# Folding the gate and noise columns of an MLP into its second weight matrix, over two steps per weight tile

## The chip, the cores and the metric

The kernel runs on one core of a Trainium2 chip, in one launch. The metric is device time in microseconds (us). The kernel before takes 1118.16 us, the median of three runs (1114.34 to 1119.37).

Five engines run their own instruction lists in order and meet only at semaphores: PE (TensorE, matmuls and transposes, which write PSUM), ACT (ScalarE, activations and copies), DVE (VectorE, elementwise work), POOL (GpSimd, here elementwise subtractions and products) and SP, which issues most DMA transfers.

## The reference, cut to what matters

Three layers follow one another on 3072 tokens (4 batches of 768) with 384 channels:

```python
state = alpha[t] * state + outer(k[t], v[t]);  y[t] = q[t] @ state   # 8 heads of 48
h = x @ w_in;  g = h * sigmoid(h);  x2 = g @ w_out                    # 384 -> 2048 -> 384
logits = x2 @ w_gate;  noise_scale = log1p(exp(x2 @ w_noise))         # 384 -> 8 experts
noisy = logits + noise_scale * noise                                  # top 2, softmax weights
out[t] = sum over its two experts of weight * relu(x2 @ w1[e]) @ w2[e]
```

The product `x2 @ w_gate` is `g @ (w_out @ w_gate)`. The kernel therefore folds the gate and noise matrices (16 columns together, called `wgn`) into `w_out` once, and the second matmul of the MLP gives 384 output columns and 16 gate and noise columns at a time.

## The kernel before

Attention works on chunks of 128 tokens, 24 of them; the MLP works on blocks of 384 tokens (three chunks), eight of them, each in 16 steps, one for each 128 rows of the hidden layer. The order of every engine's work is the order in which the program is written (`manual_schedule`): nothing is reordered.

**Attention in units.** `stage1_units` is a generator that gives a chunk in five units: unit 0 (transposed keys `kts`, score matmuls, masked scores `am`), unit 1 (`unit_kv`: new state `S`), unit 2 (first half of `y`), unit 3 (second half of `y`, copied to `xr` by ACT), unit 4 (`xr` transposed, split into `xh` and `xl`). Before the loop over MLP steps, 15 units (three chunks) run: the prelude. After that each step of the MLP runs one unit.

**Steps of the MLP.** Step m of block j runs `l1(j, m)` (nine matmuls of 384 columns), then the pointwise part `act1` (ACT `th`, DVE `gf`, ACT `gh`, POOL `gl`), then a unit of attention, then `l2(j, m-2)` (nine matmuls of 400 columns).

**Weights.** `w_in` and `w_out` come as raw 64 bit words, 64 tiles of loading in all, of which 32 are prepared: 9 in the prelude, then two in each step of block 0 (steps 0 to 10, and one in step 11). `narrow` turns a raw tile (`wraw`) into float (`wf`) by three DVE instructions (L142 to L144); `split` gives a high part by ACT and the low part by a subtraction on POOL (both L137 and L138). After each `narrow` the next raw load is issued on SP; with n buffers of `wraw` it waits for the n-th narrow before its own use.

**The fold.** A `w_out` tile that was narrowed waits in the list `folds`. `fold()` takes it: three transposes on PE (L96), a copy to `St` on ACT (L371), a product with `wgn` on PE (L374), a copy of the 16 columns to `wo_h` on ACT (L375), and the remainder to `wo_l` on DVE (L376). Then come the `th` of this step and the narrows. Folds stand at the end of each prelude chunk and right behind `l1` in each step of block 0. `St` has one buffer, which `unit_kv` also uses for its sum (L263, L264).

Of the kernel before, what the change touches and what calls it, by code (L numbers as in the profile page):

```python
# [8 lines left out]
F32 = mybir.dt.float32  # L9
F32R = mybir.dt.float32r  # L10
BF = mybir.dt.bfloat16
I32 = mybir.dt.int32
U32 = mybir.dt.uint32
AF = mybir.ActivationFunctionType
# [7 lines left out]
DM = H * D  # L22
# [10 lines left out]
KD = DM // 128  # L33
# [21 lines left out]
def attention_mlp_moe(ctx: ExitStack, tc: tile.TileContext, aqk, vt, win, wout, wgn, noise, w12,  # L55
# [3 lines left out]
    PE, DVE, ACT, POOL = nc.tensor, nc.vector, nc.scalar, nc.gpsimd  # L59
# [10 lines left out]
    s1 = s1c.enter_context(tc.tile_pool(name="s1", bufs=2, side="right"))  # L70
    stg = s1c.enter_context(tc.tile_pool(name="stg", bufs=1, side="right"))
# [3 lines left out]
    p1 = p1c.enter_context(tc.tile_pool(name="p1", bufs=3, space=PSUM))  # L75
# [3 lines left out]
    def load_chunk(c):  # L79
        t = s1.tile([PR, AL + 2 * NP * C], F32, name="aqk", bufs=3)  # L80
        if c:
            nc.sync.dma_start(t, aqk[c])
        else:
            nc.sync.dma_start(t[:, :AL], aqk[c, :, :AL])
            nc.scalar.dma_start(t[:, AL:], aqk[c, :, AL:])
        aqk_t[c] = (t[:, :AL], *[t[:, AL + i * NP * C:AL + (i + 1) * NP * C].rearrange("p (a b) -> p a b", a=NP)
                                 for i in range(2)])
        x = s1.tile([C, H, D], F32, name="v", bufs=3)
        nc.sync.dma_start(x, vt[c])
        v_t[c] = x  # L90
# [3 lines left out]
    def flip(o, x):  # L94
        n = x.shape[0]
        PE.transpose(o, x, ident[:n, :n])  # L96

    jp = stg.tile([128, DM], I32, name="wf", bufs=3)[:, :128]
    POOL.iota(jp, pattern=[[1, 128]], base=0, channel_multiplier=-1)
    ident = const.tile([128, 128], F32)  # L100
    DVE.tensor_scalar(ident, jp, 0.0, None, op0=OP.is_equal)
# [21 lines left out]
    raw = {}  # L123

    def load_w(src, m):
        t = stg.tile([128, DM, 2], I32, name="wraw", bufs=4)
        nc.sync.dma_start(t.rearrange("p n w -> p (n w)"), src[m])
        return t

    def load_win(m):  # L130
        raw["i", m] = load_w(win, m)

    def load_wout(m):
        raw["o", m] = load_w(wout, m)
# [3 lines left out]
        (eng or DVE).tensor_tensor(l, r, h.bitcast(F32), OP.subtract)  # L138

    def narrow(t, pool=None):  # L140
        f = (pool or stg).tile([128, DM], I32, name="wf", bufs=3)
        DVE.tensor_scalar(f, t[:, :, 1], 3, 0x3fffffff, op0=OP.logical_shift_left, op1=OP.bitwise_and)  # L142
        DVE.scalar_tensor_tensor(f, t[:, :, 1], -0x40000000, f, op0=OP.bitwise_and, op1=OP.bitwise_or)
        DVE.scalar_tensor_tensor(f, t[:, :, 0], 29, f, op0=OP.logical_shift_right, op1=OP.bitwise_or)  # L144
        return f.bitcast(F32)
# [54 lines left out]
    def prep_a(c):  # L200
        al = aqk_t[c][0]
        P = s1.tile([PR, NP, CP], F32, name="P", bufs=1)
        R = s1.tile([PR, NP, CP], F32, name="R", bufs=1)
        P_t[c] = (P, R)
        DVE.tensor_tensor_scan(P.rearrange("p a b -> p (a b)"), al[:, :AL - 1], past[:, :AL - 1], 1.0, OP.mult, OP.add)
        DVE.tensor_scalar(rc, P[:, :, C], 1e-30, None, op0=OP.max)
        DVE.reciprocal(rc, rc)
        for k in range(2):
            ACT.activation(junk, al, AF.Relu, bias=neg[:PR], scale=1.0 - 2.0 * k, accum_out=amx[:PR, k, c:c + 1])
        POOL.tensor_copy(rcs[:PR, c], rc)  # L210
# [122 lines left out]
    def unit():  # L333
        next(gen, None)
# [6 lines left out]
    def wl(n=1):  # L341
        for _ in range(n):
            if wloads:
                kind, m = wloads.pop(0)
                (load_win if kind == "i" else load_wout)(m)

    def wn():
        if wpreps:
            k = wpreps.pop(0)
            f = narrow(raw.pop(k))  # L350
            wl()
            return k, f
# [6 lines left out]
            if kind == "o":  # L359
                folds.append((m, f))  # L360

    folds = []

    def fold():
        while folds:
            m, f = folds.pop(0)
            p = p1.tile([128, KD, 128], F32, name="ps1")
            for k in range(KD):
                flip(p[:, k], f[:, k * 128:(k + 1) * 128])
            t = s1.tile([128, KD, 128], F32, name="St", bufs=1)  # L370
            ACT.activation(t, p, AF.Copy)  # L371
            p = p1.tile([128, 2 * E], F32, name="ps1")
            for k in range(KD):
                PE.matmul(p, t[:, k], wgn_t[:, k], start=(k == 0), stop=(k == KD - 1))  # L374
            ACT.activation(wo_h[:, m, DM:], p, AF.Copy)  # L375
            DVE.tensor_sub(wo_l[:, m, DM:], p, wo_h[:, m, DM:].bitcast(F32))  # L376

    wl(2)
    load_chunk(2)
    wl(2)  # L380
    prep_a(0)
    prep_b(0)
    prep_c(0)
# [1 line left out]
    nc.scalar.dma_start(nz, noise)  # L385
    for i in range(15):
        unit()
        if i % 5 == 4:
            fold()

    def range_load(i):
        raw["r", i] = load_w(win if i < MF else wout, i % MF)
# [245 lines left out]
    for i in range(NS + LAG):  # L638
        if i < NS:
            j, m = divmod(i, MF)  # L640
# [34 lines left out]
            if j == 0:  # L675
                fold()
                for _ in range(2):
                    w = wn()
                    step(ac)
                    wh(w)  # L680
                    step(ac)
            else:
                run(ac)
            if m < MF - 1 and j < NB - 1:
                unit()
        if i >= LAG:
            j, m = divmod(i - LAG, MF)
# [18 lines left out]
    p1 = w3c.enter_context(tc.tile_pool(name="p3", bufs=2, space=PSUM))  # L706
# [65 lines left out]
    for i in range(NS + LAG):  # L772
        if i < NS:
            q, f = divmod(i, FF)
# [5 lines left out]
            if q + 1 < len(groups):  # L780
                ne, ng = groups[q + 1]
                nt = len(GR[ng][1])
                t = f - (FF - 1 - nt)
# [16 lines left out]
        if i >= LAG:  # L800
            q, f = divmod(i - LAG, FF)
# [16 lines left out]
    with tc.If(bad != 0), ExitStack() as fc:  # L818
# [8 lines left out]
        with tc.For_i(0, B, 1) as b, tc.For_i(0, NP, 1) as pr:  # L827
            for s in range(2):
# [11 lines left out]
                for x in range(2):  # L840
                    p = pl.tile([128, 512], F32, name="ph")
# [3 lines left out]
                for e in range(D):  # L845
                    u = fw.tile([D, S], F32, name="fu")
                    w = fw.tile([D, S], F32, name="fs")
                    for x in range(2):
                        h = slice(x * HS, (x + 1) * HS)
                        p = pl.tile([128, 512], F32, name="ph")  # L850
# [14 lines left out]
        for src, dst in ((win, wt[0]), (wout, wt[1])):  # L865
            for m in range(MF):
                t = fw.tile([128, DM, 2], I32, name="fraw")
                nc.sync.dma_start(t.rearrange("p n w -> p (n w)"), src[m])
                f = narrow(t, fw)
                x = fw.tile([128, DM], F32, name="fx")  # L870
                DVE.tensor_scalar(x, t[:, :, 1].bitcast(F32), 1e4, None, op0=OP.mult)
                sq = fw.tile([128, DM], F32, name="fsq")
                DVE.tensor_tensor(sq, x, x, OP.mult)
                DVE.scalar_tensor_tensor(dst[:, m], sq, (2.0 ** -15 * 1.125 * 1e4) ** 2, f,
                                         op0=OP.is_ge, op1=OP.mult)
        with tc.For_i(0, B, 1) as b, tc.For_i(0, NCB, 1) as c:
# [5 lines left out]
            for m in range(MF):  # L882
                p = pl.tile([128, 512], F32, name="ph")
# [9 lines left out]
            p = fps.tile([128, KD, C], F32, name="ft")  # L893
# [3 lines left out]
            p = fps.tile([128, 2 * E], F32, name="fl")  # L897
# [9 lines left out]
            for e in range(E):  # L907
# [3 lines left out]
                for f in range(FF):  # L911
                    p = pl.tile([128, 512], F32, name="ph")
# [79 lines left out]
```

## Time and profile before

| what | value |
|---|---|
| median of three runs | 1118.16 us |
| profiled execution | 1118.28 us |
| its span, first to last instruction | 1116.5 us |
| PE busy over the span | 1055.8 us, 95% |
| DVE busy | 586.5 us, 53% |
| ACT busy | 395.1 us, 35% |
| POOL busy | 260.0 us, 23% |
| mean granted clock of PE | 0.979 of full speed |

The shares are means over the whole span. The stretch that the change touches is the first 165 us: the prelude up to about 64 us, and block 0 up to about 165 us. In what follows the stretch is read by itself: busy time in windows, who waited for whom in it, and the single instructions in order of time. A row of the timeline gives start, length, engine, line, operation, output and inputs, and in brackets the idle time of the engine before it and who ended that.

### The profile page before, as it was taken

To read this page: it belongs to the slowest core of one execution; us is meant where nothing else is said; L and a number is where in the kernel's file an instruction comes from. 1 tells how busy PE (TensorE), PEld (TensorE's weight loads), DVE (VectorE), ACT (ScalarE), POOL (GpSimd) and SP (SyncE) were. 2 spreads that over 40 slices of the span, in tenths; PEclk is the share of its full clock that TensorE was granted. 3 is DMA by queue.
4 is the path that set the end of the run, shared out by engine and by line. 5 is a ranking of instruction groups with operands and counts; after the bars stand their busy time and mean duration, and the time that the engine had idled before them with its cause. 6 is when DMAs were issued, how large, how long until landed. Compare 5 with 4: busy or idle time off the path is not lost. (4 is left out here: it accounts for less than half of the span.)

```text
span 1116.5 us, 16697 instructions
## 1 busy us (share of the span) xinstructions
PE 1055.8 (95%) x6323; PEld 1020.6 (91%) x6323; DVE 586.5 (53%) x1335; ACT 395.1 (35%) x837; POOL 260.0 (23%) x252
## 2 busy tenths in 40 slices
PE   4768889999999999999999998999999999999995
PEld 3668889999999999999999988999999999999995
DVE  6766664666768777686647452244333243324220
ACT  2233344333343333434335423244333333323221
POOL 4334441031301303122020222211222222221212
PEclk9998889999999999999999998999999999999998
DMA  7333387243532325222023243445444435353313
GB/s 224 95 117 91 121 276 229 88 154 117 185 104 75 118 85 167 77 85 66 1 85 111 85 135 66 103 93 151 120 86 103 101 74 129 69 123 77 42 16 38
DMA packets 55225, 119.64 MB, mean 107 GB/s; under 512 B 6640, under 2 KB 33648, under 8 KB 55136
## 3 DMA queue, kind: packets, MB, share of 16 engines
q1 hardware_dynamic: 43456, 97.23, 28.9%
q0 software_dynamic: 11264, 20.68, 10.2%
q8 instruction: 52, 0.85, 0.3%
q10 hardware_dynamic: 416, 0.58, 0.2%
q14 instruction: 37, 0.30, 0.1%
HBM read 82.22 MB, written 36.24 MB: 106 GB/s over the span
## 5 line engine op out<-in xcount | busy, mean ns | idle before, releaser
L744 PE MATMUL acc<-w3h,hx 128*128 128x384 f32 x832 | 241.9, 342 | 0.7 <-ACT y L754 0.7
L725 DVE SCALAR_TENSOR_TENSOR hx<-ph,hx 128x64 fp32r<-128x64 f32 (+1 forms) x192 | 79.2, 443 | 289.1 <-ACT hx L721 280.5
L756 POOL DMA_INDIRECT out_dram<-y,xrow x64 | 98.5, 1538 | 348.5 <-ACT y L754 284.7
L721 ACT ACTIVATE hx<-ph 128x448 fp32r<-128x448 f32 (+1 forms) x128 | 65.4, 517 | 262.8 <-PE ph L718 179.8
L744 PEld LDWEIGHTS acc<-w3h,hx 128*128 128x128 f32 x832 | 153.4, 189 | 4.3 <-ACT y L754 1.0
L744 PE MATMUL acc<-w3l,hx 128*128 128x384 f32 x448 | 150.2, 335 | 0.0
L471 PE MATMUL acc<-wo_h,gh 128*128 128x400 f32 x384 | 143.7, 374 | 0.0
L718 PE MATMUL ph<-xh,w3h 128*128 128x384 f32 (+1 forms) x384 | 136.0, 354 | 3.6 <-DVE hx L725 3.5
L718 PE MATMUL ph<-xh,w3l 128*128 128x384 f32 (+1 forms) x384 | 135.3, 352 | 0.0
L718 PE MATMUL ph<-xl,w3h 128*128 128x384 f32 (+1 forms) x384 | 135.0, 352 | 0.0
L471 PE MATMUL acc<-wo_l,gh 128*128 128x400 f32 x384 | 134.3, 350 | 0.0
L471 PE MATMUL acc<-wo_h,gl 128*128 128x400 f32 x384 | 134.1, 349 | 0.0
L444 PE MATMUL ph<-xh,win_h 128*128 128x384 f32 x384 | 131.7, 343 | 0.0
L444 PE MATMUL ph<-xl,win_h 128*128 128x384 f32 x384 | 130.5, 340 | 0.0
L444 PE MATMUL ph<-xh,win_l 128*128 128x384 f32 x384 | 130.5, 340 | 0.0
L451 ACT ACTIVATE th<-ph 128x384 f32<-128x384 f32 x128 | 62.6, 489 | 162.9 <-PE ph L444 155.1
L454 DVE SCALAR_TENSOR_TENSOR gf<-th,ph 128x384 f32<-128x384 f32 x128 | 70.5, 551 | 76.9 <-ACT th L451 75.3
L461 DVE TENSOR_TENSOR gl<-gf,gh 128x384 fp32r<-128x384 f32 x112 | 72.3, 646 | 66.3 <-ACT gh L459 61.6
L459 ACT ACTIVATE gh<-gf 128x384 fp32r<-128x384 f32 x128 | 67.2, 525 | 110.1 <-DVE gf L454 102.5
L744 PEld LDWEIGHTS acc<-w3l,hx 128*128 128x128 f32 x448 | 81.2, 181 | 0.7
L718 PEld LDWEIGHTS ph<-xh,w3h 128*128 128x128 f32 x384 | 72.5, 189 | 6.9 <-issue 4.2
L471 PEld LDWEIGHTS acc<-wo_h,gh 128*128 128x128 f32 x384 | 74.0, 193 | 2.7 <-issue 0.4
(141 smaller groups left out, 1747.0 us busy)
## 6 DMA issues: line engine op xcount, KB each, us to landing
wraw<-in_w_dram SPq DMA_DIRECT2D x64, 384.0 KB, 4.6
aqk<-in_aqk_dram SPq DMA_DIRECT2D x23, 674.2 KB, 5.4
wraw<-in_win_dram SPq DMA_DIRECT2D x32, 384.0 KB, 3.9
wraw<-in_wout_dram SPq DMA_DIRECT2D x32, 384.0 KB, 3.4
xrow<-xd SPq DMA_DIRECT2D x48, 196.5 KB, 3.4
xd<-pad SPq DMA_DIRECT2D x12, 589.5 KB, 11.4
v<-in_v_dram SPq DMA_DIRECT2D x24, 192.0 KB, 5.8
xd<-pad SPq DMA_DIRECT2D x4, 786.0 KB, 15.1
```

The lines of the kernel that those rows point to most:

```text
L444: PE.matmul(p, w[:, m, k], x[:, k], start=(n == 0), stop=(n == 3 * KD - 1))
L451: ACT.activation(th, p, AF.Tanh, scale=0.5)
L454: DVE.scalar_tensor_tensor(g, th, 1.0, p, op0=OP.add, op1=OP.mult)
L459: ACT.activation(gh, g, AF.Copy)
L461: (POOL if j == 0 else DVE).tensor_tensor(gl, g, gh.bitcast(F32), OP.subtract)
L471: PE.matmul(ACC[j][i], g[:, sl], w[:, m], start=(m == 0 and n == 0), stop=(m == MF - 1 and n == 2))
L718: PE.matmul(p[:, :N], w[:, k, fs], x[:, k], start=(n == 0), stop=(n == 3 * KD - 1))
L721: ACT.activation(hx[:, :N], p[:, :N], AF.Relu)
L725: DVE.scalar_tensor_tensor(hx[:, o:o + b - a], p[:, a:b], 0.0, hx[:, a:b].bitcast(F32), op0=OP.max, op1=OP.subtract)
L744: PE.matmul(AC3[e, g][t][:m], hx[:, o:o + m], w[:, f], start=(f == 0 and q == 0), stop=(f == FF - 1 and q == len(prods) - 1))
L756: st = POOL.indirect_dma_start(out=out, out_offset=bass.IndirectOffsetOnAxis(ap=x[:n, RW - 1:].bitcast(I32), axis=0), in_=y[a:a + n], in_o ...
```

## The change

`fold()` is cut in two. A call first finishes the tile that the call before had begun (product with `wgn`, copy to `wo_h`, remainder to `wo_l`), and then begins the next one (transposes and copy). The copy goes to a buffer of its own, `ft`, and not to `St`. The list `mids` holds the tile in between. A call takes one tile, where it took all that were in the list. In the prelude the calls move from the end of each chunk to units 0 and 2 of chunks 1 and 2. `wf` gets a fourth buffer and `wraw` gives one up, so that three raw loads are outstanding instead of four.

```diff
-    jp = stg.tile([128, DM], I32, name="wf", bufs=3)[:, :128]
+    jp = stg.tile([128, DM], I32, name="wf", bufs=4)[:, :128]
...
-        t = stg.tile([128, DM, 2], I32, name="wraw", bufs=4)
+        t = stg.tile([128, DM, 2], I32, name="wraw", bufs=3)
...
-        f = (pool or stg).tile([128, DM], I32, name="wf", bufs=3)
+        f = (pool or stg).tile([128, DM], I32, name="wf", bufs=4)
...
-    folds = []
+    folds, mids = [], []
 
     def fold():
-        while folds:
-            m, f = folds.pop(0)
-            p = p1.tile([128, KD, 128], F32, name="ps1")
-            for k in range(KD):
-                flip(p[:, k], f[:, k * 128:(k + 1) * 128])
-            t = s1.tile([128, KD, 128], F32, name="St", bufs=1)
-            ACT.activation(t, p, AF.Copy)
+        if mids:
+            m, t = mids.pop(0)
             p = p1.tile([128, 2 * E], F32, name="ps1")
             for k in range(KD):
                 PE.matmul(p, t[:, k], wgn_t[:, k], start=(k == 0), stop=(k == KD - 1))
             ACT.activation(wo_h[:, m, DM:], p, AF.Copy)
             DVE.tensor_sub(wo_l[:, m, DM:], p, wo_h[:, m, DM:].bitcast(F32))
+        if folds:
+            m, f = folds.pop(0)
+            p = p1.tile([128, KD, 128], F32, name="ps1")
+            for k in range(KD):
+                flip(p[:, k], f[:, k * 128:(k + 1) * 128])
+            t = stg.tile([128, KD, 128], F32, name="ft")
+            ACT.activation(t, p, AF.Copy)
+            mids.append((m, t))
 
     wl(2)
     load_chunk(2)
-    wl(2)
+    wl(1)
...
-        if i % 5 == 4:
+        if i % 5 in (0, 2) and i > 4:
             fold()
```

On PE, in step 3 of block 0, between the last matmul of `l1` and the second half of `y`, the order before is: transposes of the `w_out` tile (from `wf`), product with `wgn` (from `St`), `y`.

```order
 L444 MATMUL ph<-xh,win_l 128x384
 L96 MATMUL ps_694<-ident,wf 128x128 x3
 L374 MATMUL ps_700<-wgn_t,St 128x16 x3
 L275 MATMUL ps_665<-S,aqk 128x96
 L279 MATMUL ps_665<-v,am 128x48 x2
```

At the same place of the changed kernel the product comes first, and its input is `ft`.

```order
 L447 MATMUL ph<-xh,win_l 128x384
 L369 MATMUL ps_686<-wgn_t,ft 128x16 x3
 L96 MATMUL ps_692<-ident,wf 128x128 x3
 L275 MATMUL ps_657<-S,aqk 128x96
 L279 MATMUL ps_657<-v,am 128x48 x2
```

The product now belongs to the tile whose transposes stood in the step before; the transposes belong to the next one.

On ACT, from the end of step 8 to step 9 (unit 3 in between, as after step 3), before: the split of the second weight (`win_h`), the copy `xr` of unit 3, the fold's copy `St` and its `wo_h`, then step 9's `th` and first split.

```order
 L137 ACTIVATE win_h<-wf 128x384
 L282 ACTIVATE xr<-ps_1012 128x384
 L371 ACTIVATE St<-ps_1102 128x384
 L375 ACTIVATE wo_h<-ps_1108 128x16
 L451 ACTIVATE th<-ph 128x384
 L137 ACTIVATE wo_h<-wf 128x384
```

The same engine at the same place in the changed kernel:

```order
 L137 ACTIVATE win_h<-wf 128x384
 L282 ACTIVATE xr<-ps_1004 128x384
 L370 ACTIVATE wo_h<-ps_1094 128x16
 L378 ACTIVATE ft<-ps_1100 128x384
 L454 ACTIVATE th<-ph 128x384
 L137 ACTIVATE wo_h<-wf 128x384
```

`wo_h` moved ahead of the copy, so nothing of this fold stands between `xr` and it on ACT.

On PE, where the prelude ends, before: last matmul of `y`, transposes of `xr`, the whole fold of the last tile of the prelude, then the first `l1`.

```order
 L279 MATMUL ps_458<-v,am 128x48 x2
 L96 MATMUL ps_474<-ident,xr 128x128 x3
 L96 MATMUL ps_480<-ident,wf 128x128 x3
 L374 MATMUL ps_486<-wgn_t,St 128x16 x3
 L444 MATMUL ph<-xh,win_h 128x384
```

The changed kernel at the same place, up to the keys of the next chunk:

```order
 L96 MATMUL ps_478<-ident,xr 128x128 x3
 L447 MATMUL ph<-xh,win_h 128x384
 L447 MATMUL ph<-xl,win_h 128x384
 L447 MATMUL ph<-xh,win_l 128x384
 L447 MATMUL ph<-xh,win_h 128x384
 L447 MATMUL ph<-xl,win_h 128x384
 L447 MATMUL ph<-xh,win_l 128x384
 L447 MATMUL ph<-xh,win_h 128x384
 L447 MATMUL ph<-xl,win_h 128x384
 L447 MATMUL ph<-xh,win_l 128x384
 L369 MATMUL ps_494<-wgn_t,ft 128x16 x3
 L96 MATMUL ps_536<-ident,aqk 128x112 x4
```

The second half of that fold moved behind the nine matmuls of the first `l1`.

## Rows read from the trace of the kernel before

**Rows 1.** Windows: start:end, length, busy PE, PEld, DVE, ACT, POOL, clock, DMA.

```profile
60.00:165.00 105.00, 85.33 (x466) 79.77 (x467) 68.03 (x127) 39.46 (x96) 43.44 (x44) 0.85 0.49 149
165.00:200.00 35.00, 35.00 (x225) 34.60 (x225) 14.45 (x29) 13.50 (x30) 7.08 (x9) 1.00 0.71 207
```

**Rows 2.** Waits of DVE, 60 to 165 us: total, times, longest.

```profile
DVE wo_l L376 <- ACT wo_h L375: 28.7, 13, 4.8
...
DVE gf L454 <- ACT th L451: 2.0, 2, 1.7
```

**Rows 3.** Timeline of DVE: last instruction of each narrow, steps 0 to 5.

```profile
70.67 0.56 DVE L144 SCALAR_TENSOR_TENSOR wf<-wraw,wf 128x384 int32<-128x384 int32 x1
...
77.35 0.56 DVE L144 SCALAR_TENSOR_TENSOR wf<-wraw,wf 128x384 int32<-128x384 int32 x1
...
79.99 0.56 DVE L144 SCALAR_TENSOR_TENSOR wf<-wraw,wf 128x384 int32<-128x384 int32 x1
...
86.60 0.56 DVE L144 SCALAR_TENSOR_TENSOR wf<-wraw,wf 128x384 int32<-128x384 int32 x1
...
89.25 0.56 DVE L144 SCALAR_TENSOR_TENSOR wf<-wraw,wf 128x384 int32<-128x384 int32 x1
...
95.67 0.56 DVE L144 SCALAR_TENSOR_TENSOR wf<-wraw,wf 128x384 int32<-128x384 int32 x1
...
98.34 0.56 DVE L144 SCALAR_TENSOR_TENSOR wf<-wraw,wf 128x384 int32<-128x384 int32 x1
...
102.43 0.56 DVE L144 SCALAR_TENSOR_TENSOR wf<-wraw,wf 128x384 int32<-128x384 int32 x1
...
105.08 0.56 DVE L144 SCALAR_TENSOR_TENSOR wf<-wraw,wf 128x384 int32<-128x384 int32 x1
...
109.17 0.56 DVE L144 SCALAR_TENSOR_TENSOR wf<-wraw,wf 128x384 int32<-128x384 int32 x1
```

**Rows 4.** Timeline, from the end of step 3 to the first narrow of step 4.

```profile
100.26 0.84 PE L374 MATMUL ps<-wgn_t,St 128*128 128x16 f32 x6 [0.96 <-ACT St L371]
100.48 1.00 POOL L461 TENSOR_TENSOR gl<-gf,gh 128x384 fp32r<-128x384 f32 x1
...
101.36 0.17 DVE L376 TENSOR_TENSOR wo_l<-ps,wo_h 128x16 fp32r<-128x16 f32 x1 [1.86 <-ACT wo_h L375]
```

**Rows 5.** Timeline: a narrow's middle instruction beside a subtraction on POOL.

```profile
103.62 1.02 POOL L138 TENSOR_TENSOR wo_l<-wf,wo_h 128x384 fp32r<-128x384 f32 x1 [2.14 <-ACT wo_h L137]
...
103.76 1.29 DVE L143 SCALAR_TENSOR_TENSOR wf<-wraw,wf 128x384 int32<-128x384 int32 x1
```

**Rows 6.** Timeline, step 1 to step 2, behind unit 1 (`unit_kv`).

```profile
82.42 0.56 DVE L264 TENSOR_TENSOR S<-St,pcm 112x384 f32<-112x384 f32 x1
...
83.64 1.46 PE L374 MATMUL ps<-wgn_t,St 128*128 128x16 f32 x6 [4.85 <-ACT St L371]
...
84.92 0.83 POOL L220 TENSOR_TENSOR pcm<-blk,P 112x384 f32<-112x384 f32 x1
```

**Rows 7.** Timeline, step 0 to step 1, behind unit 0.

```profile
72.41 0.80 DVE L206 TENSOR_SCALAR past<-P 112x4 f32<-112x4 f32 x1
...
73.25 0.53 ACT L235 ACTIVATE kts<-ps 128x448 f32<-128x448 f32 x1
...
73.34 1.26 DVE L247 TENSOR_TENSOR am<-ps,mask 128x512 f32<-128x512 f32 x2
```

**Rows 8.** Timeline, around the end of the prelude.

```profile
42.72 0.56 DVE L295 TENSOR_TENSOR xl<-ps,xh 128x384 fp32r<-128x384 f32 x1 [1.85 <-ACT xh L294]
...
48.01 1.23 DVE L205 TENSOR_TENSOR_SCAN P<-aqk,past 112x516 f32<-112x516 f32 x1
...
64.58 0.67 PE L444 MATMUL ph<-xh,win_h 128*128 128x384 f32 x1
...
67.29 0.52 PE L444 MATMUL ph<-xh,win_l 128*128 128x384 f32 x1
```

**Rows 9.** Instructions of line 127: raw weight loads, from issue to landing.

```profile
DMA to landing us min/median/max: 2.7/3.6/9.1
```

## The prediction

> **What bounds the kernel now.** I read the windows first, because the shares of the whole span mix stages. From 165 to 200 us PE is busy for all of 35.00 us at granted clock 1.00; from 60 to 165 us it is busy for 85.33 of 105 us at 0.85 [rows 1]. So whatever time PE gains before 165 us it keeps, and the question is what holds block 0 (the stretch from 60 to 165 us). No engine is full there: DVE has 68.03 us of work, POOL 43.44, ACT 39.46 [rows 1]. It is a loop of waits. The view of waits names it: DVE stands for 28.7 us, in 13 waits, before `wo_l` (the last instruction of a fold), for ACT's `wo_h` [rows 2]. `wo_l` stands ahead of both narrows of its step, and the narrows feed ACT's splits, behind which the next fold's copy `St` stands. The timeline shows one turn of it: PE waits for `St`, runs the product at 100.26, and `wo_l` starts at 101.36 [rows 4].
>
> I measure this loop by one number. Let T be the end of the second narrow of a step. The turn is the time from T to the end of the first narrow of the next step. From there to the next T nothing changes (102.99 to 105.64, 2.65 us [rows 3]). The turns of the first five steps, by the unit of attention that runs in between, with 0.56 added to each start [rows 3]: unit 0, 71.23 to 77.91, 6.68; unit 1, 80.55 to 87.16, 6.61; unit 2, 89.81 to 96.23, 6.42; unit 3, 98.90 to 102.99, 4.09; unit 4, 105.64 to 109.73, 4.09.
>
> **The change part by part.** *Removed:* the transposes and `St` between `l1` and `wo_h`. The product of a tile is ready behind `l1`, since its copy was made a step earlier, and `wo_h` can follow ACT's split and unit work directly. *Also removed:* the shared buffer `St`. Behind unit 1 the product waited 4.85 us, because the copy could not start before `S` had read `St`, to 82.98, and it then ran 1.46 us where it takes 0.84 elsewhere [rows 4, 6]; the next turn, behind unit 2, carries the delayed PE. *Added:* nothing in instructions. The number of transposes, copies, products and remainders is the same; they are moved.
>
> *What is late next.* Not PE first, but the SBUF port that DVE and POOL contend for. A narrow's middle instruction that starts 0.14 us behind a subtraction on POOL takes 1.29 us and ends 0.41 us after POOL's end, where the third instruction, of the same form, takes 0.56 [rows 3, 5]. Behind T, POOL runs two subtractions without a gap, the second of them from 100.48 to 101.48, which is T+2.58 [rows 4]. Today the first narrow starts at T+2.6 (`wo_l` ends at 101.53, and the narrow 1.46 later, 102.99 [rows 3, 4]), so the wait for the fold covers the subtractions. Without the wait the narrow runs into them.
>
> The Trainium skill, page "SBUF — State Buffer", section "Who interferes with whom", says that a DVE instruction with two SBUF inputs contends with a GpSimd instruction that reads SBUF, and that the one that comes first keeps the port to its end. The 1.29 against 0.56 us agrees. Taken to its end (no narrow instruction gets through before POOL's second subtraction is over) it gives the low bound of the next paragraph; a free port gives the high one.
>
> New turns, each with its bounds:
> - Unit 3: `wo_l` could end at about T+1.25 (split and `xr` on ACT, some 0.9, then `wo_h` and `wo_l`), and with a free port the narrow ends at T+2.7. Blocked until T+2.58 it ends at 4.1. I take 3.6: its first instruction slips between the two subtractions, as the 0.80 us one at 72.41 did [rows 7], its second ends 0.41 after POOL, its third 0.59 later. Gain 0.5 (0 to 1.4).
> - Unit 4: `wo_l` follows `xl` at T+1.7; free 3.2, blocked 4.1, taken 4.0. Gain 0.1 (0 to 0.9).
> - Unit 2: no unit work on DVE; free 2.4, blocked 4.1, taken 3.6 as behind unit 3. PE is no longer late. Gain 2.8 (2.3 to 4.0).
> - Unit 1: `S` ends at 82.98, T+2.43; free 4.2. But POOL holds products until `pcm` ends at 85.75, T+5.2 [rows 6], and behind it a narrow needs 0.3 to 0.9. Taken 6.1; gain 0.5 (0 to 2.4).
> - Unit 0: the masked scores `am` end at 74.60, T+3.37. The product's PSUM slot is freed by `kts`, which ends at 73.78, T+2.55 [rows 7]; plus 0.84, `wo_h` and `wo_l` that is T+3.9, and the narrow ends at 5.45. Gain 1.2, or 0.6 where the product runs at 1.46. In step 1 no tile is in `mids`, so no `wo_l` stands there: 3.4 + 1.5 = 4.95, gain 1.7.
>
> Steps 1 to 11 hold two turns of each kind and a third behind unit 0: 1.7 + 2 x 1.2 + 2 x (0.5 + 2.8 + 0.5 + 0.1) = 11.9 us.
>
> *The prelude.* The folds at the ends of chunks go from DVE's path: between `xl`, which ends at 43.28, and the next scan at 48.01 lie 4.7 us for two folds [rows 8]; the single one of chunk 0 costs half of that by estimate, 2.4. In their new places a product (1.46 at the slow level [rows 6]) stands ahead of the second half of `y`, and one behind `kts` holds up the scan of chunk 2; I take 1.4 for each, 2.8 together. So the first `l1` starts some 4.3 us earlier, near 60.3. But the product of the prelude's last tile now stands behind that `l1`, which takes 3.0 us there (64.58 to 67.29, and a ninth step of 0.3 [rows 8]), then 1.4 for the product and 0.5 for `wo_h` and `wo_l`: 65.2. Today that product ends as `l1` starts, at 64.58, and `wo_l` 0.5 later, 65.1: the first narrow of step 0 starts where it did. What is left is the 1.7 us that `gf` of step 0 waits for `th` [rows 2], which is then ready. Gain 1.7. If `l1` came no earlier than now, that would be a loss of 2.7 instead.
>
> *Hidden.* One raw buffer fewer: a load now has from the end of a narrow to the start of the third one after it, at least 2.65 + 3.6 + 0.5 = 6.7 us; it takes 3.6 in the median [rows 9]. A fourth `wf` only lifts a limit. Everything behind step 11 keeps its order and shifts.
>
> Sum: 11.9 + 1.7 = 13.6 us (4.8 with the worst end of every term, 23 with a free port). The profiled execution took 1118.28 us, 0.12 above the median; 1118.2 - 13.6 = 1104.6 us.
>
> **The rivals.**
> *The port does not hold the narrows.* Turns of 2.4 to 4.2 instead of 3.6 to 6.1, 23 us, 1095 us. For it: two of a narrow's three instructions in most turns run undisturbed. Against: the row of 1.29. 0.12.
> *PE becomes the bound in block 0.* Its 85.33 us of work must fit into 105 - 13.6 = 91.4, some 94% full, and it contains long waits: behind unit 0 for `kts`, before `l1` for the `gf` of two steps earlier. After such waits the clock sits at the slower level (0.85 in the mean [rows 1]; the product takes 1.46 instead of 0.84). If 15 of today's 19.7 us of waiting remain, the stretch takes 100.3 and the gain is 4.7: 1113.5 us. For it: DVE and PE are this close. Against: the longest wait of PE, 4.85, goes, and with it a cause of slow clock. 0.22.
> *Three raw buffers are too few, and the kernel gets slower.* The slowest load took 9.1 us [rows 9], 2.4 more than the 6.7 allowed. If all 11 steps waited so long, 26 us would go against 13.6: 1131 us. It decides from landings of about 7.9 us on. Against: the median of 3.6; attention's loads stand behind the weight's in the queue. 0.10.
>
> **How the numbers follow.** The forecast's own mechanism has 0.56, range 1100 to 1110. With the free port at 0.12, PE at 0.22 and the loads at 0.10, a range from 1094 to 1117 leaves out some 0.17. About 0.5% (5.6 us) is what a measurement can tell from no change. Faster by more: 0.56 + 0.12 = 0.68; within: 0.22; slower: 0.10.
>
> **What would show it.** In the profile after, DVE's wait for `wo_h` should fall from 28.7 to about 5 us, while the first narrow's instructions grow to 1 us and more behind units 1, 2 and 3. The turns should read near 5, 6.1, 3.6, 3.6, 4.0. PE should be full from about 151 us on. The forecast is wrong if those turns stay near 6.6 behind unit 2, if DVE waits for `wraw` loads, or if PE's busy time in block 0 grows.

## The result

| kernel | median, us | runs | ratio to before, 95% interval |
|---|---|---|---|
| before | 1118.37 (1114.34 to 1119.37) | 4 | 1 |
| changed | 1100.44 (1098.52 to 1102.43) | 4 | 0.9847 [0.9816, 0.9877] |

The change makes the kernel 17.9 us faster by the medians (by the ratio, 1.53%, it is 17.1); 13.6 were forecast. The 1100.44 us lie at the lower edge of the range of 1100 to 1110 that the forecast gave its own mechanism. The profiled execution took 1100.98 us, with a span of 1099.2 (before 1116.5) and a mean clock of 0.988.

The profile after, windows as in [rows 1] (start:end, length, then busy PE, PEld, DVE, ACT, POOL, clock, DMA share, GB/s):

```profile
60.00:147.70 87.70, 74.05 (x448) 70.76 (x448) 74.69 (x123) 36.27 (x90) 44.37 (x43) 0.90 0.54 163
147.70:182.70 35.00, 35.00 (x227) 34.63 (x227) 14.31 (x28) 13.69 (x31) 6.50 (x8) 1.00 0.85 246
...
66.56:142.31 75.75, 62.10 (x380) 59.33 (x380) 68.58 (x111) 32.67 (x81) 38.70 (x38) 0.90 0.53 160
```

PE is full from 147.7 us on, 17.3 us earlier than the window of [rows 1] that is full. The `l2` of step 12 starts at 147.60 us, before at 164.78: nearly the whole difference of the spans (17.3) is made by then. The last row runs from T of step 0 to the first narrow of step 11. The same stretch of before is this window:

```profile
71.23:160.38 89.15, 71.86 (x395) 67.57 (x395) 59.95 (x112) 33.80 (x82) 37.46 (x38) 0.83 0.50 150
```

It went from 89.15 to 75.75 us, a gain of 13.4. PE's busy time in it fell by 9.8 us, at a granted clock of 0.90 instead of 0.83. These two windows do not cut PE's list at the same places; from the first matmul of `l1` in step 1 to that in step 12 (70.50 to 160.06 before, 64.80 to 143.82 after), with the same `l1` and `l2` in between, it fell from 72.27 to 65.37, by 6.9 us.

The clock column has to be read with care: it stands at 1.00 up to about 80 us before and 75 us after, although the matmuls of the first `l1` start 0.32 us apart there ([rows 8]: eight of them from 64.58 to 67.29), as they do later at 0.50 (after, at 80.5 us), while at 1.00 they start 0.17 us apart (after, at 87 us). So the means of 0.83, 0.85 and 0.90 are too high, by an amount that the column does not give.

DVE's busy time rose from 59.95 to 68.58: the narrows now take longer themselves. The waits of DVE from 60 to 165 us, in the form of [rows 2], show the other side of that:

```profile
DVE wo_l L371 <- ACT wo_h L370: 13.6, 8, 4.3
DVE gf L457 <- ACT th L454: 8.9, 5, 3.5
```

The wait for the fold fell from 28.7 to 13.6 us. Three of its eight are not of steps 1 to 11: 4.33 stands in step 0, and 2.27 and 3.76 stand behind step 11, where PE is the bound. In steps 1 to 11 it is 3.2 us. The 8.9 us of `gf` stand behind step 11 too: between 66.56 and 142.31 us DVE has no wait for `th`. No wait for `wraw` is in DVE's list.

The timeline of DVE answers to [rows 3]: the last instruction of the narrows of step 0 (second narrow), and steps 2, 3 and 4.

```profile
66.00 0.56 DVE L144 SCALAR_TENSOR_TENSOR wf<-wraw,wf 128x384 int32<-128x384 int32 x1
...
79.00 1.07 DVE L144 SCALAR_TENSOR_TENSOR wf<-wraw,wf 128x384 int32<-128x384 int32 x1
...
82.17 0.56 DVE L144 SCALAR_TENSOR_TENSOR wf<-wraw,wf 128x384 int32<-128x384 int32 x1
...
85.88 0.56 DVE L144 SCALAR_TENSOR_TENSOR wf<-wraw,wf 128x384 int32<-128x384 int32 x1
...
88.53 0.56 DVE L144 SCALAR_TENSOR_TENSOR wf<-wraw,wf 128x384 int32<-128x384 int32 x1
...
92.27 0.56 DVE L144 SCALAR_TENSOR_TENSOR wf<-wraw,wf 128x384 int32<-128x384 int32 x1
```

82.73 to 86.44 is the turn behind unit 2, 3.71; 89.09 to 92.83 the one behind unit 3, 3.74. All turns up to step 11, read in this way:

| turn behind | before | forecast | after |
|---|---|---|---|
| unit 0, steps 1, 6, 11 | 6.68, 7.13, 6.63 | 4.95, then 5.45 or 6 | 4.80, 5.53, 4.88 |
| unit 1 | 6.61, 6.44 | 6.1 | 6.05, 5.55 |
| unit 2 | 6.42, 6.29 | 3.6 | 3.71, 3.74 |
| unit 3 | 4.09, 4.09 | 3.6 | 3.74, 3.73 |
| unit 4 | 4.09, 4.12 | 4.0 | 3.74, 3.74 |

T of step 0 itself is at 66.56, before at 71.23: 4.7 us earlier, where 1.7 were forecast. This is the term that was too small. Some 0.5 us of the 4.7 is chance: the first scan, which waits for the landing of its input, started at 5.76 us here and at 6.29 before. The changed kernel, run again (below), started it at 6.42 and has T at 67.24. Counted from that scan, T is 4.1 us earlier in both executions.

What happens inside a turn is seen behind unit 2, in order of time on all engines:

```profile
82.90 0.73 PE L369 MATMUL ps<-wgn_t,ft 128*128 128x16 f32 x6
83.36 1.00 POOL L138 TENSOR_TENSOR win_l<-wf,win_h 128x384 fp32r<-128x384 f32 x1 [1.64 <-ACT win_h L137]
...
83.88 0.17 DVE L371 TENSOR_TENSOR wo_l<-ps,wo_h 128x16 fp32r<-128x16 f32 x1 [1.15 <-ACT wo_h L370]
83.98 0.60 DVE L142 TENSOR_SCALAR wf<-wraw 128x384 int32<-128x384 int32 x1
84.32 1.11 POOL L464 TENSOR_TENSOR gl<-gf,gh 128x384 fp32r<-128x384 f32 x1
84.61 1.23 DVE L143 SCALAR_TENSOR_TENSOR wf<-wraw,wf 128x384 int32<-128x384 int32 x1
```

The product no longer waits for a copy: it starts 0.17 us behind T and takes 0.73. Before, at this place, it started 3.7 us behind T (89.81):

```profile
93.51 0.84 PE L374 MATMUL ps<-wgn_t,St 128*128 128x16 f32 x6 [0.64 <-ACT St L371]
```

`wo_l` is over at T+1.3, and the narrow starts beside POOL: its first instruction gets through where POOL's first subtraction ends, its second ends at 85.84, 0.41 us after POOL's second one. That is the turn as it was worked out, instruction by instruction.

### The profile page after: what moved, and what is told of

Read it like the earlier page. It is cut to its first block, busy times and chain, and to the rows that moved or that the text cites. A ratio compares the mean times of both kernels' runs of the same rounds, so it can differ in the third digit from the quotient of the medians.

```text
span 1099.2 us, 16698 instructions
## 1 busy us (share of the span) xinstructions
PE 1047.7 (95%) x6323; PEld 1015.4 (92%) x6323; DVE 595.6 (54%) x1335; ACT 393.3 (36%) x837; POOL 260.5 (24%) x252
## 4 chain that ended last, share of the span: by engine, by line
PE 51%; issue 24%; DMA 13%; DVE 8%; POOL 2%; ACT 1%; POOLq 0%; DVEq 0%; ACTq 0%
PE acc L474 19%; PE ph L447 17%; DMA out_dram<-y,xrow 12%; PE ps L279 3%; DVE wf L143 3%; PE acc L747 3%; PE ph L721 3%; PE ps L96 2%; PE ps L243 2%; PE ps L275 2%; PE ps L256 1%; DVE wf L142 1%; POOL out_dram L759 1%; DVE wf L144 1%; DVE P L205 1%
## 6 DMA issues: line engine op xcount, KB each, us to landing
xd<-pad SPq DMA_DIRECT2D x12, 589.5 KB, 13.4
```

## The experiments

The runs were made in three sets, each kernel beside runs of before on the same chip (medians of before: 1118.27, 1118.51 and 1118.11 us). "Block" below means T of step 0 to the end of the first narrow of step 11: 89.15 us before, 75.75 after.

**The buffers alone.** Before, with `wf` 4, `wraw` 3 and one load fewer ahead:

```diff
-        t = stg.tile([128, DM, 2], I32, name="wraw", bufs=4)
+        t = stg.tile([128, DM, 2], I32, name="wraw", bufs=3)
...
-        f = (pool or stg).tile([128, DM], I32, name="wf", bufs=3)
+        f = (pool or stg).tile([128, DM], I32, name="wf", bufs=4)
...
-    wl(2)
+    wl(1)
```

> The kernel before with only the buffer counts of the change (wf 4, wraw 3, one raw load fewer at the start). Theory (the gain comes from where the halves of the fold stand): no change, within 2 us of before, and DVE's wait for the fold's wo_h stays at 28 to 29 us between 60 and 165 us. Rival (the fourth wf buffer lifts a limit): 3 us or more faster. Second rival (three raw loads are too few): DVE waits for wraw, 3 us or more slower.

Measured: 1117.64 us, ratio 0.9995 [0.9987, 1.0004]. DVE still waits 28.0 us for `wo_h`. The buffers of the raw and narrowed weights neither help nor harm by themselves, in the old order.

**A copy of its own, the order as before.** The fold stays whole and at its old places; besides the buffer counts of the run above, only its copy leaves `St`:

```diff
-            t = s1.tile([128, KD, 128], F32, name="St", bufs=1)
+            t = stg.tile([128, KD, 128], F32, name="ft")
```

> The kernel before with the buffer counts of the change and the fold's copy in its own buffer ft, but the fold whole and at its old places. Theory (two parts: the shared St buffer makes PE late behind unit 1, the in-order chain costs the rest): the turn behind unit 2 falls from 6.4 to about 4.1 us, that behind unit 1 from 6.5 to about 6.0, the others stay; 5 to 6 us faster in all, about 1112.5. Rival (only the split counts): no change, 1118. Second rival (the shared buffer was the whole cost): 13 us or more faster.

Measured: 1113.74 us, ratio 0.9957 [0.9944, 0.9970]; the block takes 83.59, 5.6 less than before. Behind unit 1 the turns are 6.06 and 5.55, and behind unit 2 3.99 and 3.98, while those behind unit 3 (4.09) stay, and those behind unit 0 are 7.27, 7.13 and 6.47 (the first 0.6 longer than before, the last 0.2 shorter). Its timeline at the place of [rows 6], ACT and PE:

```profile
82.02 0.49 ACT L371 ACTIVATE ft<-ps 128x384 f32<-128x384 f32 x1 [0.21 <-PE ps L96]
...
82.56 0.84 PE L374 MATMUL ps<-wgn_t,ft 128*128 128x16 f32 x6 [0.64 <-ACT ft L371]
```

The copy runs before `S` is done, and the product waits 0.64 us instead of 4.85. So 5.6 of the block's 13.4 us come from sharing no buffer with `unit_kv`; the other 7.8 need the order in two steps.

**The two places apart.** First the block alone: in the prelude the folds are made whole at the ends of the chunks.

```diff
-        if i % 5 in (0, 2) and i > 4:
-            fold()
+        if i % 5 == 4:
+            while folds or mids:
+                fold()
```

> The change with the prelude's folds whole and at the end of each chunk as before; split over two steps only in block 0. Theory (prelude and block add up): the turns of block 0 as in the changed kernel (75.7 us from T of step 0 to the first narrow of step 11, 89.2 before), T of step 0 as before at about 71 us; 13 to 14 us faster, about 1105. Rival (a later start of block 0 is made up by PE or the port): all 17 us.

Then the prelude alone: in block 0 each call does the whole fold, with `St`.

```diff
-    def fold():
+    def fold(whole=False):
...
-            t = stg.tile([128, KD, 128], F32, name="ft")
+            t = s1.tile([128, KD, 128], F32, name="St", bufs=1) if whole else stg.tile([128, KD, 128], F32, name="ft")
             ACT.activation(t, p, AF.Copy)
             mids.append((m, t))
+            if whole:
+                fold()
...
-                fold()
+                fold(True)
```

> The change with the folds of block 0 whole and copied to St as before; split and moved only in the prelude. Theory: T of step 0 is 4 us earlier (about 66.8 where the first scan starts at 5.8 to 6.3), the turns of block 0 as before (6.7, 6.6, 6.4, 4.1, 4.1); 4 us faster, about 1114. Rival (block 0 takes it back, since the loop of waits there sets its own pace): 0 to 1 us faster.

Measured: block alone 1104.61 us, ratio 0.9880 [0.9865, 0.9894]; its block takes 75.76, and T of step 0 stands at 71.11, as before. Prelude alone 1114.89 us, ratio 0.9962 [0.9948, 0.9975]; its block takes 89.33, and T of step 0 stands at 66.32. The gains, 13.7 and 3.4, add up to 17.1, nearly the whole 17.9, so no dependence of the two places shows in the times. Within the second run the single turns are not all as before (behind unit 0 7.63 and 6.69, behind unit 2 7.10 and 6.94); only their sum is.

In the second run T is 4.9 us earlier, but the median is only 3.4 lower. The trace shows where the rest went: the `l2` of step 12 starts at 160.06, 4.7 us earlier than before, but its nine matmuls start 0.33 us apart (clock 0.50 from 161 to 163 us) where before they start 0.18 apart, and the next `l1` starts at 163.07 against 166.51, 3.4 us earlier. The prediction assumed that the time PE gains before 165 us is kept; here the slower level of the clock took 1.3 us of it back.

The first run also speaks on PE. Its window of the block reads:

```profile
71.11:146.87 75.76, 59.38 (x378) 56.82 (x379) 68.86 (x112) 32.81 (x81) 38.75 (x38) 0.93 0.52 162
```

PE is busy for 2.7 us less than in the changed kernel, at 0.93 instead of 0.90, and the block is not shorter by it. So PE's busy time does not set its length here.

**POOL's subtractions taken away.** In the changed kernel POOL writes zeros in place of the low parts of the weights and of block 0's `g` (these low parts are left out of the computation), so that of its work in block 0 only the products of the units and one small copy still read. Lines 142 to 144 are 145 to 147 here.

```diff
-        (eng or DVE).tensor_tensor(l, r, h.bitcast(F32), OP.subtract)
+        if eng is POOL:
+            POOL.memset(l.bitcast(F32), 0.0)
+        else:
+            DVE.tensor_tensor(l, r, h.bitcast(F32), OP.subtract)
...
-        (POOL if j == 0 else DVE).tensor_tensor(gl, g, gh.bitcast(F32), OP.subtract)
+        if j == 0:
+            POOL.memset(gl.bitcast(F32), 0.0)
+        else:
+            DVE.tensor_tensor(gl, g, gh.bitcast(F32), OP.subtract)
```

> The changed kernel with POOL's subtractions of block 0 and of the weights (low parts, and gl of block 0) replaced by a memset of the same tile, which reads nothing from SBUF: the low parts are left out of the computation, the instruction counts and waits stay. Theory (what holds the narrows behind T is POOL reading SBUF): the narrow's middle instruction falls from a mean of 1.16 us to below 0.75, the turns behind units 2 and 3 from 3.7 to about 2.7, the time from a narrow's end to the next T from 2.65 to about 1.9; some undisturbed rows remain long behind unit 1, where POOL's two products stay. Rival (the instructions wait for something else, a semaphore or a DMA): 1.16 us and turns of 3.7 stay.

Measured: 1088.15 us, ratio 0.9730 [0.9710, 0.9749]. The group of the narrow's middle instruction from 57 us on (count, busy time and mean ns), first of the changed kernel (before, 60 to 165 us: the same 23, 878 ns), then of this one:

```profile
L143 DVE SCALAR_TENSOR_TENSOR wf<-wraw,wf 128x384 int32<-128x384 int32 x23 | 26.7, 1162 | 0.8
```

```profile
L146 DVE SCALAR_TENSOR_TENSOR wf<-wraw,wf 128x384 int32<-128x384 int32 x23 | 14.8, 641 | 0.8
```

One narrow of it, undisturbed, on DVE behind unit 2:

```profile
82.51 0.35 DVE L145 TENSOR_SCALAR wf<-wraw 128x384 int32<-128x384 int32 x1
82.90 0.56 DVE L146 SCALAR_TENSOR_TENSOR wf<-wraw,wf 128x384 int32<-128x384 int32 x1
83.49 0.56 DVE L147 SCALAR_TENSOR_TENSOR wf<-wraw,wf 128x384 int32<-128x384 int32 x1
```

So it is POOL's reading that makes the narrows long, as the forecast had it. Where POOL still reads, the instruction stays long. Behind unit 0 it now runs beside the product `aqk` (on POOL from 69.79 to 71.07):

```profile
70.07 1.41 DVE L146 SCALAR_TENSOR_TENSOR wf<-wraw,wf 128x384 int32<-128x384 int32 x1
```

The block takes 65.97 us, 9.8 less than after. Only 4.4 of that lie in the eleven turns (together 44.8 against 49.2), the other 5.4 in the second narrows of the steps, which take 1.9 to 2.0 us in eight of ten. In the first round the turns behind units 2 and 3 are 2.29 and 2.67, as expected. In the second they are 4.83, longer than the 3.74 of the changed kernel, and 3.59, because there `wo_h` comes late (waits of 3.20 and 1.35 us). The one of 3.20:

```profile
113.27 0.17 DVE L374 TENSOR_TENSOR wo_l<-ps,wo_h 128x16 fp32r<-128x16 f32 x1 [3.20 <-ACT wo_h L373]
```

There PE is behind: the matmuls of its `l1` start 0.32 us apart until 111.5. The three turns behind unit 0 got longer as well (5.14, 6.14 and 5.60 against 4.80, 5.53 and 4.88). Freed from the port, DVE meets the fold again.

**The last product of the prelude ahead of `l1`.** In the changed kernel this product stood behind the first `l1`, and DVE waited 4.33 us for it. One half call ahead of the loop over the steps moves it forward:

```diff
+    hold, folds[:] = folds[:], []
+    fold()
+    folds[:] = hold
```

> The changed kernel with the product, wo_h and wo_l of the prelude's last tile ahead of the first l1 (behind the transposes of xr) instead of behind it. Theory (in the change the first narrow of step 0 stands behind nine matmuls at the slow clock): l1 starts some 1 us later, near 58.5, the first narrow starts at about 59 instead of 62.4, T of step 0 falls from 66.6 to about 64.6, limited by th; 2 us faster than the changed kernel, 1098.5. Rival (PE sets the pace there): no gain, or 1 us slower.

Measured: 1098.44 us, ratio 0.9821 [0.9808, 0.9835]. T of step 0 stands at 64.70 instead of 66.56, and the block is as long as in the changed kernel (75.80). Its timeline on ACT and DVE:

```profile
58.25 0.18 ACT L370 ACTIVATE wo_h<-ps 128x16 fp32r<-128x16 f32 x1 [0.60 <-PE ps L369]
...
58.47 0.17 DVE L371 TENSOR_TENSOR wo_l<-ps,wo_h 128x16 fp32r<-128x16 f32 x1 [0.23 <-ACT wo_h L370]
58.56 0.35 DVE L142 TENSOR_SCALAR wf<-wraw 128x384 int32<-128x384 int32 x1
```

The narrow starts at 58.56 instead of 62.38, 3.8 us earlier, and T gains 1.9 of it: the `th` of step 0 is late next, as expected. `gf` waits 1.74 us for it, and it follows the last matmul of `l1`.

**The remainder behind the first narrow.** `wo_l` of block 0 is issued on DVE after the first narrow instead of ahead of it:

```diff
-    folds, mids = [], []
-
-    def fold():
+    folds, mids, late = [], [], []
+
+    def fold(wait=False):
...
-            DVE.tensor_sub(wo_l[:, m, DM:], p, wo_h[:, m, DM:].bitcast(F32))
+            late.append(lambda m=m, p=p: DVE.tensor_sub(wo_l[:, m, DM:], p, wo_h[:, m, DM:].bitcast(F32)))
+            if not wait:
+                late.pop(0)()
...
-                fold()
+                fold(True)
...
+                    if late:
+                        late.pop(0)()
```

> The changed kernel with wo_l of block 0 placed on DVE behind the first narrow of its step instead of ahead of it. Theory (behind T the port and not the fold's wait sets the turn, except where the narrow can now start before POOL's subtraction): behind unit 2 the narrow starts at T and the turn falls from 3.7 to about 2.4; behind unit 3 from 3.7 to between 3.0 and 3.7; behind unit 1 and 4 no change; behind unit 0 from 5.5 to 4.9; T of step 0 about 1 us earlier. 3 to 6 us faster than the changed kernel, about 1096. Rival (the wait for wo_h, 13.6 us in 8 waits, is the bound): 12 us or more faster, 1088. Second rival (PE is the bound by now): no gain.

Measured: 1096.64 us, ratio 0.9812 [0.9795, 0.9829]; block 72.82, 2.9 shorter. Behind unit 2 the turns are 2.14, behind unit 0 4.8, behind unit 3 3.43. Behind unit 1 they are 5.46 and 5.44 where no change was expected: 0.6 and 0.1 less. T of step 0 is at 66.18, 0.4 earlier, and 1.0 earlier when counted from the first scan (at 6.40 here). The timeline behind unit 2, on DVE and POOL, with T at 81.90:

```profile
81.81 0.35 DVE L142 TENSOR_SCALAR wf<-wraw 128x384 int32<-128x384 int32 x1
...
82.20 0.56 DVE L143 SCALAR_TENSOR_TENSOR wf<-wraw,wf 128x384 int32<-128x384 int32 x1
...
82.53 1.10 POOL L138 TENSOR_TENSOR win_l<-wf,win_h 128x384 fp32r<-128x384 f32 x1 [1.65 <-ACT wo_h L370]
...
82.79 1.25 DVE L144 SCALAR_TENSOR_TENSOR wf<-wraw,wf 128x384 int32<-128x384 int32 x1
```

The narrow now starts before POOL does, and two of its three instructions run at full speed. The wait for the fold was thus still on the path in the changed kernel, by 1.15 us behind unit 2.

Not all of this is kept. The eleven turns are 5.3 us shorter together (43.9 against 49.2), but the second narrows are 2.4 us longer (28.9 against 26.5). Behind unit 2 DVE comes to the `gf` of its step before POOL is done with `gl`:

```profile
84.96 0.55 DVE L459 SCALAR_TENSOR_TENSOR gf<-th,ph 128x384 f32<-128x384 f32 x1 [0.83 <-POOL gl L466]
```

**Both, and the change beside it.** The last two edits in one kernel:

> The two edits together: the prelude's last product ahead of the first l1, and wo_l of block 0 behind the first narrow. Theory: they add up where they don't meet; in step 0 both take the same wait away, so 4 to 7 us faster than the changed kernel, about 1095. Rival (PE fills up): not faster than either edit alone.

Measured: 1095.40 us, ratio 0.9799 [0.9778, 0.9819]; T of step 0 at 64.73, block 72.83, each as with one edit alone. The intervals of the two single edits (up to 0.9835 and 0.9829) overlap that of the change (0.9816 to 0.9877), so the times alone do not settle either; the rows show the steps, and the pair was measured once more. In the third set the changed kernel and this one ran again on one chip:

> The changed kernel once more, beside the two below on the same chip. Expected by every theory: 1100.4 us, 18 us faster than before.

> The two edits together once more (last product of the prelude ahead of the first l1, wo_l of block 0 behind the first narrow). Theory: 4 to 6 us faster than the changed kernel on the same chip, 1095. Rival (the difference lay between the chips' runs): within 2 us of the changed kernel.

Measured: the changed kernel 1101.38 us (1100.06 to 1102.31), 0.9845 [0.9832, 0.9859]; the one with both edits 1096.16 (1095.64 to 1099.01), 0.9801 [0.9788, 0.9815]. The two edits are worth 5.2 us more than the change, which itself is 16.7 us faster than before in this set. The profiled execution of the pair is here its slowest (1099.01), and its block takes 74.37: in step 6 the second narrow takes 5.09 instead of 3.54, with PE at 0.32 us for a matmul of `l1` until 102.5 and the product and `th` late behind it.

**`gl` on DVE too.** The same kernel, with the subtraction of block 0's pointwise part taken from POOL:

```diff
-        (POOL if j == 0 else DVE).tensor_tensor(gl, g, gh.bitcast(F32), OP.subtract)
+        DVE.tensor_tensor(gl, g, gh.bitcast(F32), OP.subtract)
```

> The two edits, and gl of block 0 on DVE, where blocks 1 to 7 have it already. It takes a read of 1.0 to 1.7 us from POOL's port and adds 0.65 us of work to DVE in each of 16 steps. Theory (the port sets the turns): behind unit 1 the turn falls from 5.4 to about 4.5, behind unit 3 from 3.4 to about 3.1, behind units 0 and 4 it grows by up to 0.6; in all between 2 us faster and 1 us slower than the two edits. Rival (DVE's own work is the bound): 8 us or more slower.

Measured: 1093.59 us (1090.91 to 1097.11), ratio 0.9779 [0.9759, 0.9799], the best of all kernels here that compute the whole output, 24.5 us faster than before. Its interval overlaps that of the kernel without this edit a little, so the last 2.6 us are likely rather than settled. The block takes 71.67, against 72.83 and 74.37 in the two runs of the pair. Turns are shorter behind units 3 (3.2) and 4 (3.0, where a growth was expected), longer behind units 0 (5.3) and 2 (2.7), where DVE now has the subtraction in its own queue. Behind unit 1 they read 5.74 and 5.23 where 4.5 was expected, a miss: unit 1's own two products on POOL are still there. Added up, the turns are not shorter at all (44.6 against 43.9 in both runs of the pair). What is gained lies in the second narrows, 27.0 against 29.0 and 30.5: `gf` has no wait for `gl` any more, and no second narrow is longer than 2.9.

## Why the prediction was right, and where it was off

*The bound in block 0.* Right. Without the wait the block shortens by 13.4 us where 11.9 were forecast. By kinds of turns, forecast against measured: step 1 1.7 and 1.88; the later two behind unit 0 2.4 and 3.35; unit 1 1.0 and 1.45; unit 2 5.6 and 5.26; unit 3 1.0 and 0.71; unit 4 0.2 and 0.73. The largest misses are unit 0 and unit 4. The later turns behind unit 0 were worked out from the first one before (6.68), but the one of step 6 was 7.13; after, it is 5.53 where 5.45 was worked out, and the one of step 11 is 4.88, since there the product ran ahead of T (at 137.02) and not behind `kts`. Unit 4 was taken as nearly blocked (4.0 of 4.1) and ran like unit 3. The sign that the instructions grow to 1 us and more holds for all three only behind unit 1; behind units 2 and 3 it holds for the middle one (1.23 and 1.25).

*The shared buffer.* Right: the copy of its own, alone, gives the shorter turns behind units 1 and 2 and leaves the others as they were.

*The port.* Right in its mechanism: without POOL's reads the middle instruction falls from 1162 to 641 ns on average. The rival of a free port is refuted by the same rows. But its price was not where the forecast put it. It had 9.4 us between a blocked and a free port in the turns (23 less 13.6); the run shows 4.4 there, and 5.4 in the second narrows, which had been taken as fixed at 2.65 us. A port that is wholly free was not tested: the products of unit 1 still read in that run.

*PE as the bound.* Refuted for the block as a whole. It took PE's 85.33 us as given (they are 93% of 91.4, not 94), but for the same `l1` and `l2` PE's busy time fell by 6.9 us at a higher clock. Its waits fell as well, from 17.3 to 13.7 (89.15 - 71.86 and 75.75 - 62.10). In the run of the block alone PE is busy for less time still, and the block has the same length. In single steps PE at the slow level can still be what is late, as step 6 in the second run of the pair shows. Why the clock of this stretch rose was not tested by itself.

*Three raw loads.* Refuted: the buffers alone change nothing, and with the shorter turns no wait for `wraw` appears. The rival was also priced from a row that does not belong to the block: the 9.1 us of [rows 9] are of a load behind 165 us. Of the loads issued between 60 and 165 us the slowest landed in 3.6 us before and in 4.5 after, well within the 6.7 allowed.

*The prelude.* This term failed in its size: 1.7 us forecast, 4.7 measured. The steps behind the first `l1` were right. From its start to the first narrow the forecast had 4.9 us, and it took 4.96:

```profile
57.40 0.56 DVE L295 TENSOR_TENSOR xl<-ps,xh 128x384 fp32r<-128x384 f32 x1 [1.48 <-ACT xh L294]
57.42 0.69 PE L447 MATMUL ph<-xh,win_h 128*128 128x384 f32 x1 [0.58 <-ACT xh L294]
...
60.74 1.29 PE L369 MATMUL ps<-wgn_t,ft 128*128 128x16 f32 x6
...
62.28 0.17 DVE L371 TENSOR_TENSOR wo_l<-ps,wo_h 128x16 fp32r<-128x16 f32 x1 [4.33 <-ACT wo_h L370]
62.38 0.35 DVE L142 TENSOR_SCALAR wf<-wraw 128x384 int32<-128x384 int32 x1
```

What was wrong is the start of `l1`: 57.42, 7.2 us earlier than the 64.58 of [rows 8], where 4.3 were forecast. The gaps at the chunks' ends, in the timeline of DVE:

```profile
40.65 0.56 DVE L295 TENSOR_TENSOR xl<-ps,xh 128x384 fp32r<-128x384 f32 x1 [0.73 <-ACT xh L294]
41.13 1.22 DVE L205 TENSOR_TENSOR_SCAN P<-aqk,past 112x516 f32<-112x516 f32 x1
...
57.40 0.56 DVE L295 TENSOR_TENSOR xl<-ps,xh 128x384 fp32r<-128x384 f32 x1 [1.48 <-ACT xh L294]
```

From the start of `xl` to the next scan it was 5.29 us behind chunk 1 (42.72 to 48.01) and is 0.48; behind chunk 0 it went from 2.47 to 0.47. That is 6.8 of the 7.1 forecast. The step that failed is the third gap, which the sum left out: a whole fold stood between the last `xl` (62.62) and the first `l1` (64.58), 1.96 us, and now `l1` starts 0.02 behind `xl`. It had been counted only as the old time of the product, not as a delay of `l1`. Besides, the two delays were taken as 1.4 us each and measured 0.46 in chunk 1 and 1.66 in chunk 2 (from the scan to `xl`: 15.07 and 16.27, against 14.61 in both before). 6.8 + 1.9 - 2.1 is 6.6; the remaining 0.5 is the first scan, which started at 5.76 instead of 6.29 behind the landing of its input. That part is luck, not the change. The run with the prelude alone, whose first scan started at 5.88, gives a T of step 0 4.9 earlier (4.5 when counted from the scan) and a median 3.4 lower.

*The wait for `wo_h`.* The forecast said about 5 us in all and it is 13.6. The steps of block 0 that it was worked out for hold 3.2; what was missing is the 4.33 of step 0, which its own sum contained, and the two behind step 11.

## What to carry to other kernels

Where engines run their lists in order, cutting a chain in two and doing its halves a step apart can take the chain's latency off the path without removing any instruction; what is gained is bounded by what the wait was hiding, here POOL's reads beside DVE's. When a piece of work is moved out of several places, write down for each place what stood behind it, on every engine, and count each: the one left out here was the one at the seam between two stages. And before cutting a chain, look whether its copy shares a buffer with other work: one changed buffer name gave more than a quarter of the whole gain (0.43 of 1.53%).

## What had not been expected of the hardware

A run of operations on POOL without gaps does not always shut DVE out until it ends. Behind unit 1 of the changed kernel each instruction of a narrow gets in once for each operation of POOL and ends 0.2 to 0.4 us after it:

```profile
75.91 1.39 POOL L464 TENSOR_TENSOR gl<-gf,gh 128x384 fp32r<-128x384 f32 x1
...
76.45 1.07 DVE L142 TENSOR_SCALAR wf<-wraw 128x384 int32<-128x384 int32 x1
77.26 1.29 POOL L217 TENSOR_TENSOR aqk<-aqk,P 112x512 f32<-112x512 f32 x1
77.55 1.42 DVE L143 SCALAR_TENSOR_TENSOR wf<-wraw,wf 128x384 int32<-128x384 int32 x1
78.52 1.15 POOL L220 TENSOR_TENSOR pcm<-blk,P 112x384 f32<-112x384 f32 x1
79.00 1.07 DVE L144 SCALAR_TENSOR_TENSOR wf<-wraw,wf 128x384 int32<-128x384 int32 x1
```

A narrow of 1.5 us takes 3.6 in this way; it is the longest turn that is left, and taking `wo_l` out of its way gained only 0.1 to 0.6 us. It is no rule, however: in the prelude of the same kernel one instruction was held over two operations of POOL and ended 0.4 us after the second. What decides between the two was not tested.

```profile
50.95 0.83 POOL L220 TENSOR_TENSOR pcm<-blk,P 112x384 f32<-112x384 f32 x1 [3.98 <-DVE S L264]
51.11 2.04 DVE L143 SCALAR_TENSOR_TENSOR wf<-wraw,wf 128x384 int32<-128x384 int32 x1
51.74 0.99 POOL L138 TENSOR_TENSOR wo_l<-wf,wo_h 128x384 fp32r<-128x384 f32 x1
```

In the run without POOL's subtractions, whose zeros are written and nothing is read, a narrow's first instruction was still held, and an instruction with two inputs was not:

```profile
77.93 0.56 DVE L147 SCALAR_TENSOR_TENSOR wf<-wraw,wf 128x384 int32<-128x384 int32 x1
78.14 0.41 POOL L468 MEMSET gl<- 128x384 f32 x1
...
78.86 0.41 POOL L139 MEMSET win_l<- 128x384 f32 x1
78.87 1.71 DVE L145 TENSOR_SCALAR wf<-wraw 128x384 int32<-128x384 int32 x1
...
79.95 0.41 POOL L139 MEMSET win_l<- 128x384 f32 x1
80.61 0.56 DVE L146 SCALAR_TENSOR_TENSOR wf<-wraw,wf 128x384 int32<-128x384 int32 x1
```

1.71 us over four writes of zeros, where it takes 0.35 alone. The third, with two inputs, ran in 0.56 beside such a write; the second (L146) has the same form. The Trainium skill, page "SBUF — State Buffer", section "Who interferes with whom", has both halves: a DVE instruction with two SBUF inputs contends with a GpSimd (POOL) instruction that reads SBUF and not with one that only writes it, while DVE in a mode with two ports, which `tensor_scalar` can enter, contends with GpSimd, and there the page makes no such exception. The trace agrees with both, by the 0.56 and the 1.71 us; that this instruction ran in such a mode is concluded from its length alone. So the run without the subtractions freed two of a narrow's three instructions, and not the first.
